# Strassen's scheme on two pairs of token blocks instead of one, with weights in stages of two chunks, in a kernel of attention and two expert layers

## The chip, the cores and the metric

The kernel runs on one core of a Trainium2 chip. The metric is the device time of the whole program in microseconds (us); lower is better. Times of several executions of the kernel before are given below, and one of its executions was profiled.

## The reference

Attention with a window of 32 over 512 local positions and 32 global ones (4 batches, 8 heads, head size 64), then two layers without gates, each a product, a squared ReLU and a product:

```python
def _moe_ref(x, w_in, w_out):          # x: 2176 tokens x 512 here, d_ff = 2048
    h = x @ w_in
    r = np.maximum(h, 0.0)
    return ((r * r) @ w_out).astype(np.float32)

attn_out = _attn_ref(...)              # softmax over window and global keys
x = attn_out.transpose(0, 2, 1, 3).reshape(B * S, H * D)     # 2176 x 512
x = _moe_ref(x, moe_w_in, moe_w_out)
return _moe_ref(x, moe2_w_in, moe2_w_out)
```

The weights arrive as 64-bit floats and are narrowed on the chip.

## The kernel before

**Precision.** Each product of the layers is made of three matmuls of a rounded part and a remainder: `three()` issues hi x hi, hi x lo and lo x hi (lines L575, L576, L577), and every operand that is used is first split in a high part (`xh`, `gh`, `whi`, `th`) by ScalarE and a low part (`xl`, `gl`, `wlo`, `tl`) by a subtraction. "A three" below is one such group.

**Tiling.** Tokens lie in five blocks of 256, 512, 512, 512 and 384 columns (blocks 0 to 4). The hidden size of 2048 is cut in 16 chunks of 128 per layer; the model size of 512 is four pieces `k` (into `w_in`) or `d` (out of `w_out`). A wave is four chunks of both weights, so there are 8 waves, wave 0 beside the attention. For one chunk, a block that goes the plain way needs 4 threes into `h` and 4 threes out of `w_out`.

**Strassen's scheme.** Blocks 1 and 2 are a pair from wave 1 on. For two chunks, `products` makes the same four results from 7 products of two threes, 14 threes instead of 16. For it `sums` combines two weight chunks into two more operands (slots `sa`, `sb`), and `tsums` combines the pair's inputs into three more (`t`, at the start of each layer). One running sum is kept in PSUM, copied out three times by ScalarE (`keep`) and added to by VectorE (`plus`, L707).

**Activation.** A plain result takes ScalarE's ReLU and square (L596, L597), VectorE's exact square (L599) and VectorE's remainder (L233). A staged result of the pair takes VectorE's square (L589), ScalarE's copy to `gh` (L591) and the remainder. Results of `w_out` are added into `y` by VectorE (L626): a plain block once in a wave, the pair's blocks twice.

**Weights.** `weight` loads a chunk (512 KB), and VectorE and ScalarE rebuild 32-bit floats from the halves of the 64-bit ones (L488 to L500); `split` writes `whi` and `wlo` of a slot. There are 12 slots.

**Order.** All instructions are given to a planner (`Plan`) with costs, a priority and what they read and write; it simulates the engines and always takes the ready instruction of the lowest priority number. The order that it prints is fixed when the program is built, and each engine then runs its own list in order. `CFG` holds the priorities, the order of the blocks in each wave, and a string per kind of step that deals its instances to engines in turn (A ScalarE, D VectorE, P GpSimd). In the attention part TensorE fills its pauses with wave 0.

Of the kernel before, what the change touches and what calls it, by code (L numbers as in the profile page):

```python
# [10 lines left out]
F32 = mybir.dt.float32  # L11
# [15 lines left out]
BLOCKS = [[0], [1, 2], [3, 4], [5, 6], [7]]  # L27
NB = [256, 512, 512, 512, 384]
OFF = [0, 256, 768, 1280, 1792]
UNIT_POS = {u: (b, 256 * j) for b, us in enumerate(BLOCKS) for j, u in enumerate(us)}  # L30
WAVES = 4
NSLOT = 12
PB = (1, 2)
CFG = {'sg': 'AAA',
 'tl': 'D',
 'tp': [495.69, 306.05],
 'order': ['340W', '3W04', 'W403', '4W30', 'W043', '0W43', '3W40'],
 'EARLY': 8,
 'ck': 'PPPP',
 'cq': 'P',  # L40
 'lo': 'DDD',
 'nm': 'APA',
 'ev': 'A',
 'yc': 'A',
 'wl': 'DDDD',
 'gl': 'D',
 'xh': 'AAA',
 'glob': [6, 7, 13, 15, 19, 26, 27, 29],
 'w0': -7.103,
 'w1': 56229.445,  # L50
 'moe': [850.402, 480.622, -326.592, -124.726, -387.48],
 'step': [0.1043, 0.0123, 0.0591, 0.0383, 0.0372],
 'NK': 3,
 'NQ': 2,
 'wa': 'ADDA',
 'lid': -6.29,
 'lmk': -11.49,
 'gbuf': '01',
 'lead': 14112208.283,
 'NM': 2,  # L60
 'NS': 3,
 'NPT': 2,
 'NV': 2,
 'lag': 6,
 'NR': 3,
 'NWR': 1,
 'NWT': 3,
# [4 lines left out]
 'O': ['O0']}  # L72
# [129 lines left out]
def kernel(ctx: ExitStack, tc: tile.TileContext, kl, ql, vl, gk, gv, win, wout, msk, idn, out):  # L202
# [47 lines left out]
    gh = tiles(big, "gh", 4, [128, 512], F32R)  # L250
    gl = tiles(big, "gl", 4, [128, 512], F32R)
# [24 lines left out]
    late_opened, tt_ = [], []  # L276
# [24 lines left out]
    def pair(j, prio):  # L301
# [31 lines left out]
        visit(P, scores, (M, ML, HQ, LQ), tuple(sk), 0.767)  # L333
# [48 lines left out]
        b, c0 = UNIT_POS[u]  # L382

        def after(P):
            split_out(b, [h2], xh[b][:, h2, c0:c0 + 256], xl[b][:, h2, c0:c0 + 256], ok, bank[ok][:, 0:256], 256, P)

        add("PE", 0.924, P(), pv, A + (("pt", pbs[0]), ("pt", pbs[1]), ("v", vb)), (ok,), mode="V")
        after(P)

    waiting = []  # L390

    def visit(P, scores, reads, writes, cost):

        if scores:
            add("PE", cost, P(), scores, ("arena",) + reads, writes, mode="S")
# [8 lines left out]
    def glob(n, prio):  # L404
# [3 lines left out]
        k, v = (yflat[3], yflat[4]) if gb == 0 else (yflat[2], yflat[1])  # L408
# [62 lines left out]
        c0 = 256 + 32 * bb  # L471
# [60 lines left out]
    def weights(w, prio, prio_step, step=1e-3):  # L532
# [16 lines left out]

        def chunk(kind, i):  # L550
            s, a = slot()
            res[kind].append(s)
            if prio_step:
                q[0] = prio + prio_step * (len(res["in"]) + len(res["out"]) - 1)
            return weight((win if kind == "in" else wout)[4 * w + i], s, P, a)

        if w == 0:
            for kind in ("in", "out"):
                for i in range(4):
                    chunk(kind, i)  # L560
            return res
        for p in range(2):
            t = [chunk("in", 2 * p + i) for i in range(2)]
            ss = [slot() for _ in range(2)]
            sums(t[0], t[1], [s for s, _ in ss], P, dict(ss))
            res["sum"].append([s for s, _ in ss])
            for i in range(2):
                chunk("out", 2 * p + i)
# [15 lines left out]
    def activate(P, f, nb, src, S, staged):  # L584

        a, l = gh[f][:, 0:nb], gl[f][:, 0:nb]
        if staged:
            r, R = src, S
# [4 lines left out]
        else:  # L593
            r, R = staging()
            r = r[:, 0:nb]
# [3 lines left out]
            add("DVE", dve(nb), P(), lambda: nc.vector.scalar_tensor_tensor(  # L599
                out=r, in0=src, scalar=0.0, in1=r, op0=ALU.max, op1=ALU.mult), (S,), (R,))  # L600
# [5 lines left out]
    def second(P, b, fs, slots, late, dfirst, stages):  # L606
# [11 lines left out]
        def finish(d):  # L618
# [3 lines left out]
            if begin:  # L622
                first = {1: (("gv", 1),), 2: (("gk", 1), ("gp", 1)), 3: (("gk", 0), ("gp", 0)), 4: (("gv", 0),)}.get(b, ())
# [3 lines left out]
            if end and layer == 0:  # L627
                if b == PB[1] and d < 2:
                    return
# [25 lines left out]
    def moe(W, layer, wave, b, prio, late, step=1e-3, free=False):  # L655
        nb = NB[b]
        c3 = 3 * pe_r(nb)
        q = [prio]

        def P():  # L660
            q[0] += step
            return q[0]

        for f in range(4):
            slot = W["in"][f]
            hk = take("h", CFG["h"] + CFG["S"] if late else CFG["h"])
            hp = bank[hk][:, 0:nb]
            for k in range(KD):
                add("PE", c3, P(), lambda k=k, slot=slot, hp=hp: three(
                    hp, wv(whi, slot)[:, k, :], wv(wlo, slot)[:, k, :], xh[b][:, k, :], xl[b][:, k, :], k == 0, k == KD - 1),  # L670
                    (("w", slot), ("x", b, k)), (hk,))
            activate(P, f, nb, hp, hk, False)
        second(P, b, range(4), W["out"], late, not late, (layer, wave == 0, wave == WAVES - 1))
        if free:
            release(*W["in"], *W["out"])
# [3 lines left out]
    tkey = lambda n, i: ("x", PB[1], i) if n == 1 else ("T", n, i)  # L679
# [238 lines left out]
```

## Time and profile before

| | |
|---|---|
| median of 3 runs | 892.65 us (891.47 to 893.81) |
| the profiled execution | 893.89 us |
| its span, from first to last instruction | 892.0 us |
| TensorE busy | 871.2 us |
| VectorE busy | 685.5 us |
| ScalarE busy | 428.9 us |
| GpSimd busy | 64.6 us |
| mean granted TensorE clock | 0.998 of full speed |

The busy time of an engine counts the time in which at least one of its instructions is under way; instructions of one engine overlap a little, so it is less than the sum of their durations. The profiled execution lies 1.24 us above the median of the runs.

### The profile page before, as it was taken

Reading aid. Unit: us, or ns where it says so; the run is one execution under the profiler, and the core shown is the slowest. Engines: PE = TensorE matmul, PEld = TensorE weight load, DVE = VectorE, ACT = ScalarE, POOL = GpSimd, SP = SyncE. Lnnn points to the kernel's source line nnn. Section 1 sums busy time; section 2 is a strip of 40 time slices with the busy share of each in tenths; the row PEclk is TensorE's granted clock in tenths of the full one; section 3 lists DMA queues with packets and bytes.
Section 4 is the critical chain, followed back from the end, with each engine's and each line's share of the span. In section 5 each row is a group of like instructions: output and inputs, shape, how many; then the busy total and the mean of one; then the engine's idle time right before and its main releaser. Section 6 shows DMA issues by size and latency. Waiting matters only on the chain.

```text
span 892.0 us, 14332 instructions
## 1 busy us (share of the span) xinstructions
PE 871.2 (98%) x5332; PEld 752.9 (84%) x5332; DVE 685.5 (77%) x1584; ACT 428.9 (48%) x996; POOL 64.6 (7%) x119
## 2 busy tenths in 40 slices
PE   5989999999999999999999999999999999999998
PEld 4878887788789988889989998889899888988898
DVE  5878889653797788897999988847885988494653
ACT  5879899984552333333435544425323432232221
POOL 3323243310000000000000000000000000000000
PEclk9999999999999999999999999999999999999999
DMA  8568644410202102111210112201111211011021
GB/s 307 178 209 273 206 127 136 129 32 1 71 1 71 48 0 63 56 48 49 71 47 25 48 48 71 71 25 32 64 48 48 58 61 48 25 47 48 1 96 60
DMA packets 28071, 67.93 MB, mean 76 GB/s; under 512 B 3168, under 2 KB 12512, under 8 KB 28000
## 3 DMA queue, kind: packets, MB, share of 16 engines
q1 hardware_dynamic: 28000, 67.01, 23.8%
q8 instruction: 42, 0.69, 0.3%
q14 instruction: 29, 0.24, 0.1%
HBM read 62.54 MB, written 4.46 MB: 75 GB/s over the span
## 4 chain that ended last, share of the span: by engine, by line
PE 92%; DVE 3%; DMA 2%; ACT 2%; issue 1%; SPq 0%; POOL 0%; POOLq 0%; DVEq 0%; ACTq 0%
PE h L575 7%; PE h L576 7%; PE h L577 7%; PE PT L575 6%; PE PT L577 6%; PE PT L576 6%; PE S L575 6%; PE S L577 6%; PE S L576 6%; PE Y L575 5%; PE Y L577 4%; PE Y L576 4%; PE O L378 4%; PE O L575 3%; PE O L577 3%; PE O L576 3%
## 5 line engine op out<-in xcount | busy, mean ns | idle before, releaser
L575 PE MATMUL h<-xh,whi 128*128 128x512 f32 (+2 forms) x298 | 108.2, 363 | 0.0
L576 PE MATMUL h<-xl,whi 128*128 128x512 f32 (+2 forms) x298 | 105.3, 353 | 0.0
L577 PE MATMUL h<-xh,wlo 128*128 128x512 f32 (+2 forms) x298 | 105.2, 353 | 0.0
L233 DVE TENSOR_TENSOR gl<-r,gh 128x512 fp32r<-128x512 f32 (+2 forms) x160 | 96.8, 608 | 9.9 <-ACT gh L591 7.9
L577 PE MATMUL PT<-gh,wlo 128*128 128x512 f32 (+2 forms) x288 | 102.6, 356 | 0.0
L575 PE MATMUL PT<-gh,whi 128*128 128x512 f32 (+2 forms) x288 | 102.6, 356 | 0.0
L576 PE MATMUL PT<-gl,whi 128*128 128x512 f32 (+2 forms) x288 | 102.6, 356 | 0.0
L524 ACT ACTIVATE whi<-wt 128x512 fp32r<-128x512 f32 x92 | 57.3, 627 | 60.9 <-DVE wt L500 38.9
L233 DVE TENSOR_TENSOR wlo<-wt,whi 128x512 fp32r<-128x512 f32 x92 | 62.8, 686 | 26.1 <-ACT whi L524 25.9
L575 PE MATMUL S<-xh,whi 128*128 128x512 f32 (+2 forms) x230 | 80.2, 349 | 1.0 <-DVE r L599 1.0
L577 PE MATMUL S<-xh,wlo 128*128 128x512 f32 (+2 forms) x230 | 80.1, 348 | 0.0
L576 PE MATMUL S<-xl,whi 128*128 128x512 f32 (+2 forms) x230 | 80.1, 348 | 0.0
L575 PE MATMUL Y<-gh,whi 128*128 128x512 f32 (+2 forms) x208 | 76.8, 369 | 2.5 <-ACT y L218 2.5
L577 PE MATMUL Y<-gh,wlo 128*128 128x512 f32 (+2 forms) x208 | 74.7, 359 | 0.0
L576 PE MATMUL Y<-gl,whi 128*128 128x512 f32 (+2 forms) x208 | 74.7, 359 | 0.0
L596 ACT ACTIVATE r<-h 128x512 f32<-128x512 f32 (+2 forms) x67 | 34.3, 512 | 73.4 <-PE h L577 73.0
L597 ACT ACTIVATE gh<-r 128x512 fp32r<-128x512 f32 (+2 forms) x118 | 63.9, 542 | 10.4 <-PE O L577 6.6
L347 ACT ACTIVATE s<-s,mn 128x224 f32<-128x224 f32 x128 | 60.3, 474 | 17.0 <-DVE mn L342 16.1
L575 PEld LDWEIGHTS h<-xh,whi 128*128 128x128 f32 x298 | 56.4, 189 | 8.3 <-issue 0.3
L576 PEld LDWEIGHTS h<-xl,whi 128*128 128x128 f32 x298 | 56.5, 190 | 6.4 <-DVE xl L400 0.2
L577 PEld LDWEIGHTS h<-xh,wlo 128*128 128x128 f32 x298 | 56.4, 189 | 6.4
L596 ACT ACTIVATE r<-S 128x512 f32<-128x512 f32 (+2 forms) x51 | 25.7, 504 | 73.8 <-PE S L577 65.7
(109 smaller groups left out, 2011.5 us busy)
## 6 DMA issues: line engine op xcount, KB each, us to landing
wraw<-win SPq DMA_DIRECT2D x32, 512.0 KB, 3.6
wraw<-wout SPq DMA_DIRECT2D x32, 512.0 KB, 3.6
v<-vl SPq DMA_DIRECT2D x32, 224.0 KB, 2.8
rk<-kl SPq DMA_DIRECT2D x32, 192.0 KB, 3.5
y<-gk SPq DMA_DIRECT2D x8, 672.0 KB, 5.4
y<-gv SPq DMA_DIRECT2D x8, 640.0 KB, 6.7
rq<-ql SPq DMA_DIRECT2D x32, 128.0 KB, 3.0
out<-y SPq DMA_DIRECT2D x12, 256.0 KB, 2.0
```

What stands on the lines that cost most here:

```text
L233: add("DVE", dve(n), prio, lambda: nc.vector.tensor_tensor(out=get(out_), in0=get(a), in1=get(b), op=ALU.subtract), reads, writes, lock=True)
L347: add("Activation", 0.48, P(), lambda t=t, sb=sb: nc.scalar.activation(out=st[sb][:, t, :], in_=st[sb][:, t, :], func=AF.Exp, bias=mn[sb][ ...
L378: nc.tensor.matmul(out=bank[ok][64 * e:64 * e + 64, 128 * t:128 * t + 128], lhsT=vt[vb][:, 128 * k + 64 * e:128 * k + 64 * e + 64], rhs=pt ...
L524: nc.scalar.activation(out=whi[slot], in_=tf, func=AF.Copy)
L575: nc.tensor.matmul(out=out_, lhsT=hi, rhs=xhi, start=start, stop=False, skip_group_check=again)
L576: nc.tensor.matmul(out=out_, lhsT=hi, rhs=xlo, start=False, stop=False, skip_group_check=again)
L577: nc.tensor.matmul(out=out_, lhsT=lo, rhs=xhi, start=False, stop=stop, skip_group_check=again)
L596: add("Activation", act(nb), P(), lambda: nc.scalar.activation(out=r, in_=src, func=AF.Relu), (S,), (R,))
L597: add("Activation", act(nb) + 0.04, P(), lambda: nc.scalar.activation(out=a, in_=r, func=AF.Square), (R,), (("gh", f),))
```

## The change

Blocks become 256, 512, 512, 448 and 448 columns. Blocks 1 and 2 are pair A, blocks 3 and 4 pair B, and both go through `w_in` by `products`; block 0 alone goes the plain way. After wave 0, which keeps its four plain chunks, there are 14 stages of two chunks (6 in the first layer, 8 in the second) instead of 7 waves of four. A stage has the three parts 0, A and B in an order of its own, and the `w_out` part of a pair's second block is issued after the next part's products (`pending`). Every block's `w_out` results are now added to `y` once in a stage. Weight slots are 8 instead of 12, staging tiles (`r`) 8 instead of 3, temporary weight tiles 4 instead of 3, tiles of transposed probabilities (`pt`) 6 instead of 2, and tiles for `k` 2 instead of 3. The ring of GpSimd's own DMAs, which the kernel does not use, shrinks to 256 bytes. `CFG` deals steps anew: 8 of the 32 roundings of `k` (`ck`) go to ScalarE and 16 to VectorE, 21 of the 32 remainders of `k` (`lo`) go to GpSimd, 27 of the evictions of attention results (`xh`) go to VectorE, and the exact square goes to ScalarE for all staged results and for four plain ones out of five.

```diff
-BLOCKS = [[0], [1, 2], [3, 4], [5, 6], [7]]
-NB = [256, 512, 512, 512, 384]
-OFF = [0, 256, 768, 1280, 1792]
+NB = [256, 512, 512, 448, 448]
+OFF = [0, 256, 768, 1280, 1728]
-WAVES = 4
-NSLOT = 12
-PB = (1, 2)
+PAIRS = {"A": (1, 2), "B": (3, 4)}
+STAGES = KF // 2
-CFG = {'sg': 'AAA',
- 'order': ['340W', '3W04', 'W403', '4W30', 'W043', '0W43', '3W40'],
+CFG = {'sg': 'A',
- 'ck': 'PPPP',
+ 'ck': 'APDD',
- 'lo': 'DDD',
+ 'lo': 'PDP',
- 'xh': 'AAA',
- 'glob': [6, 7, 13, 15, 19, 26, 27, 29],
- 'w0': -7.103,
+ 'xh': 'DADDA',
+ 'glob': [0, 2, 5, 8, 16, 17, 23, 27],
+ 'w0': 5694.227,
- 'NK': 3,
+ 'NK': 2,
- 'NPT': 2,
+ 'NPT': 6,
- 'NR': 3,
+ 'NR': 8,
- 'NWT': 3,
+ 'NWT': 4,
+ 'order': ['0AB', 'A0B', 'AB0', '0BA', 'A0B', '0BA', 'B0A', 'B0A', 'B0A', 'A0B', '0AB', 'A0B', '0AB', 'BA0'],
+ 'NSLOT': 8,
+ 'gf': 'AAAAD',
+ 'gs': 'A'}
...
-            for j in range(3):
-                tt_.append([lp.tile([128, 2, 512], F32R, name=f"t{k}{j}") for k in "hl"])
+            for g, (b, _) in PAIRS.items():
+                for n in (2, 3, 4):
+                    tt_[g, n] = [lp.tile([128, 2, NB[b]], F32R, name=f"t{g}{k}{n}") for k in "hl"]
...
-        if staged:
-            r, R = src, S
+        r, R = (src, S) if staged else staging()
+        r = r[:, 0:nb]
+        if staged and pick("gs") == "D":
...
-            add("DVE", dve(nb), P(), lambda: nc.vector.scalar_tensor_tensor(
-                out=r, in0=src, scalar=0.0, in1=r, op0=ALU.max, op1=ALU.mult), (S,), (R,))
+            if staged or pick("gf") == "A":
+                add("Activation", act(nb) + 0.04, P(), lambda: nc.scalar.activation(out=r, in_=r, func=AF.Square), (), (R,))
+            else:
+                add("DVE", dve(nb), P(), lambda: nc.vector.scalar_tensor_tensor(
+                    out=r, in0=src, scalar=0.0, in1=r, op0=ALU.max, op1=ALU.mult), (S,), (R,))
...
-    for lw in range(1, 2 * WAVES):
-        layer, wave = divmod(lw, WAVES)
-        order = CFG["order"][lw - 1]
-        for n, j in enumerate(order):
-            prio, last = 100 * lw + 10 * n, n == len(order) - 1
-            if j == "W":
-                wino(W, layer, wave, prio, free=last)
-            else:
-                moe(W, layer, wave, int(j), prio, True, free=last)
-        if lw == WAVES - 1:
-            tsums(100 * lw + CFG["tp"][1], True)
-        if lw + 1 < 2 * WAVES:
-            W = weights(lw + 1, 1000, 0)
+            W = weights((KF * layer + 2 * p, KF * layer + 2 * p + 1), 1000, 0, True)
+            if stage == 0:
+                for i, g in enumerate(PAIRS):
+                    tsums(g, CFG["tp"][i], False)
...
+                if j == "0":
+                    for i in range(2):
+                        first(P, W, 0, i, mine[i], True)
+                    rest, blocks = None, (0,)
+                else:
+                    rest, blocks = products(W, j, P, mine), PAIRS[j]
+                    if j == pairs[-1]:
+                        release(*W["sum"])
+                if n == len(order) - 1:
+                    release(*W["in"])
+                if pending:
+                    pending()
+                if rest:
...
+                    rest(P, theirs)
+                    second(P, blocks[0], mine, W["out"], True, True, stages)
...
-    nc = _bacc.Bacc("TRN2", target_bir_lowering=False, num_devices=1)
+    nc = _bacc.Bacc("TRN2", target_bir_lowering=False, num_devices=1, dynamic_dma_scratch_size=256)
```

Three places in the order of instructions show what moves. The first is TensorE's list in the middle of the layers, where block 3 meets `w_in`. `h0`, `h1`, `S0` and `S1` are PSUM banks; the number behind the underscore tells tiles of one program apart. Before, a chunk (`whi4`, then `whi5`) meets the block's own parts `xh3` and `xl3`, 512 columns wide:

```order
L575 MATMUL S0_143<-xh3_67,whi4_98 128x512
L576 MATMUL S0_143<-xl3_72,whi4_98 128x512
L577 MATMUL S0_143<-xh3_67,wlo4_106 128x512
L575 MATMUL S1_144<-xh3_67,whi5_99 128x512
L576 MATMUL S1_144<-xl3_72,whi5_99 128x512
L577 MATMUL S1_144<-xh3_67,wlo5_107 128x512
```

In the changed kernel, in the middle of a part B, a combined weight (slot 2) meets the pair's combined input `tB2` and then block 4's own:

```order
L565 MATMUL S1_153<-tBh2_2837,whi2_102 128x448
L566 MATMUL S1_153<-tBl2_2838,whi2_102 128x448
L567 MATMUL S1_153<-tBh2_2837,wlo2_110 128x448
L565 MATMUL h1_150<-xh4_68,whi2_102 128x448
L566 MATMUL h1_150<-xl4_73,whi2_102 128x448
L567 MATMUL h1_150<-xh4_68,wlo2_110 128x448
```

For two chunks the blocks 3 and 4 had 16 threes each here; they now have 14 together with the same columns as one block of 448, and all their matmuls are 448 wide.

The second place is the start of TensorE's list, behind the scores of the first pair of heads (L330, L334 scores; L365, L369 transposes; L382 product with `v`; L422 scores of the global queries). Before, the scores of the second pair follow at once, then the transposes of the first, then the third pair's scores:

```order
L330 MATMUL S0_143<-hk1_116,lq1_122 128x224
L330 MATMUL S1_144<-hk1_116,lq1_122 128x224
L330 MATMUL S0_143<-lk1_118,hq1_120 128x224
L330 MATMUL S1_144<-lk1_118,hq1_120 128x224
L365 MATMUL PT0_145<-ident_139,s0_123 112x128 x4
L365 MATMUL PT1_146<-ident_139,s1_124 112x128 x4
L330 MATMUL S0_143<-hk0_115,hq0_119 128x224
L330 MATMUL S1_144<-hk0_115,hq0_119 128x224
```

In the changed kernel the first pair's last scores are followed by scores of a global step and by the first pair's own transposes and product:

```order
L334 MATMUL S0_152<-lk0_122,hq0_124 128x224
L334 MATMUL S1_153<-lk0_122,hq0_124 128x224
L422 MATMUL S0_152<-y1_75 128x272 x2
L369 MATMUL PT0_154<-ident_148,s0_128 112x128 x4
L369 MATMUL PT1_155<-ident_148,s1_129 112x128 x4
L422 MATMUL S1_153<-y1_75 128x272 x2
L382 MATMUL O0_156<-pt0_131,v0_137 64x128
L382 MATMUL O0_156<-pt1_132,v0_137 64x128
```

The global steps have moved ahead, and the second pair's scores stand behind the first pair's product. On the DMA queue the first weight chunk, which was the 9th load, is now the 17th, behind four loads of the global steps.

The third place is VectorE's list where the first layer ends and the inputs of the second are combined (`y` are the layer's results, `tl` and `xl` remainders, L759 and L725 the sums of `tsums`, L599 the exact square). Before, the one pair's sums stand between the work of a plain block of 384 columns:

```order
L759 TENSOR_TENSOR y2_76<-y2_76,y1_75 128x512
L633 TENSOR_TENSOR xl2_71<-y2_76,xh2_66 128x512
L233 TENSOR_TENSOR tl1_2735<-y2_76,th1_2734 128x512
L599 SCALAR_TENSOR_TENSOR r2_89<-S0_143,r2_89 128x384
L233 TENSOR_TENSOR xl2_71<-y2_76,xh2_66 128x512
L233 TENSOR_TENSOR gl0_83<-r2_89,gh0_79 128x384
```

In the changed kernel pair B's sums stand between the work of pair A's last part of the first layer, and pair A's sums follow some 40 instructions later:

```order
L725 TENSOR_TENSOR y4_78<-y4_78 128x448
L625 TENSOR_TENSOR xl4_73<-y4_78,xh4_68 128x448
L695 TENSOR_TENSOR r0_87<-r0_87,S0_152 128x512
L235 TENSOR_TENSOR tBl3_2840<-y4_78,tBh3_2839 128x448
L725 TENSOR_TENSOR y4_78<-y4_78,y3_77 128x448
L725 TENSOR_TENSOR y3_77<-y3_77,y4_78 128x448
L725 TENSOR_TENSOR y4_78<-y4_78 128x448
L725 TENSOR_TENSOR y3_77<-y3_77 128x448
L235 TENSOR_TENSOR gl0_83<-r0_87,gh0_79 128x512
```

There are two sets of such sums instead of one, and of the exact squares one is left in VectorE's list around them.

## Rows read from the trace of the kernel before

**Rows 1.** The page: span, and each engine's busy time, share and instructions.

```profile
span 892.0 us, 14332 instructions
PE 871.2 (98%) x5332; PEld 752.9 (84%) x5332; DVE 685.5 (77%) x1584; ACT 428.9 (48%) x996; POOL 64.6 (7%) x119
```

**Rows 2.** Busy time by stretch: length, engines' busy us (instructions), TensorE clock, DMA share, GB/s.

```profile
0.00:20.00 20.00, 9.59 (x57) 7.14 (x59) 11.19 (x40) 9.43 (x28) 6.85 (x16) 1.00 0.90 313
0.00:215.50 215.50, 201.29 (x1895) 163.82 (x1895) 155.84 (x633) 173.44 (x527) 64.60 (x119) 0.99 0.52 165
260.00:888.00 628.00, 626.98 (x3237) 552.36 (x3236) 491.15 (x883) 232.89 (x427) 0.00 (x0) 1.00 0.15 48
450.00:500.00 50.00, 50.00 (x277) 45.67 (x276) 48.77 (x92) 24.77 (x47) 0.00 (x0) 1.00 0.10 32
```

**Rows 3.** TensorE's waits over the whole span: us in total, times, longest.

```profile
PE S L330 <- DVE mn L342: 6.3, 3, 5.3
...
PE O L378 <- DMA v<-vl: 2.7, 1, 2.7
PE Y L575 <- ACT y L218: 2.5, 4, 0.7
PE S L575 <- DVE r L599: 1.0, 1, 1.0
```

**Rows 4.** Timeline of TensorE at three widths: start us, duration, line, tiles.

```profile
319.73 0.39 PE L575 MATMUL h<-xh,whi 128*128 128x512 f32 x1
319.96 0.39 PE L576 MATMUL h<-xl,whi 128*128 128x512 f32 x1
...
432.17 0.33 PE L575 MATMUL Y<-gh,whi 128*128 128x384 f32 x1
432.35 0.33 PE L576 MATMUL Y<-gl,whi 128*128 128x384 f32 x1
...
406.09 0.28 PE L575 MATMUL h<-xh,whi 128*128 128x256 f32 x1
406.21 0.28 PE L576 MATMUL h<-xl,whi 128*128 128x256 f32 x1
```

**Rows 5.** Groups by line, one shape apart: the pair's combined inputs on TensorE.

```profile
L575 PE MATMUL S<-th,whi 128*128 128x512 f32 x42 | 16.3, 389 | 0.0
L575 PE MATMUL h<-th,whi 128*128 128x512 f32 x42 | 16.3, 389 | 0.0
```

**Rows 6.** Groups by line, one shape apart, and timeline: prices off TensorE.

```profile
L626 DVE TENSOR_TENSOR y<-y,PT 128x256 f32<-128x256 f32 x12 | 4.6, 418 | 0.0
L589 DVE SCALAR_TENSOR_TENSOR r<-r 128x512 f32<-128x512 f32 x42 | 28.8, 686 | 0.4
L488 DVE TENSOR_SCALAR wt<-wraw 128x512 uint32<-128x512 uint32 x64 | 27.2, 426 | 21.7 <-DMA wraw<-win 13.7 <-DMA wraw<-wout 7.7
L597 ACT ACTIVATE gh<-r 128x512 fp32r<-128x512 f32 x54 | 34.0, 630 | 1.4 <-PE Y L577 0.5
L226 POOL TENSOR_SCALAR hk<-rk 128x384 fp32r<-128x384 f32 x32 | 18.4, 574 | 56.6 <-PE S L330 28.5 <-issue 13.1 <-DMA rk<-kl 7.6
...
472.56 0.68 DVE L626 TENSOR_TENSOR y<-y,Y 128x512 f32<-128x512 f32 x1
473.16 0.68 DVE L626 TENSOR_TENSOR y<-y,PT 128x512 f32<-128x512 f32 x1
```

**Rows 7.** Timeline of the start: first steps of GpSimd, VectorE and TensorE.

```profile
6.76 0.40 POOL L226 TENSOR_SCALAR hq<-rq 128x256 fp32r<-128x256 f32 x1
6.77 0.80 DVE L233 TENSOR_TENSOR lk<-rk,hk 128x384 fp32r<-128x384 f32 x1 [1.91 <-POOL hk L226]
10.75 0.39 DVE L342 CUSTOM_DVE_ANT_0 s<-S,masks 128x224 f32<-128x224 f32 x1 [2.84 <-DMA masks<-msk]
12.00 0.55 DVE L233 TENSOR_TENSOR lk<-rk,hk 128x384 fp32r<-128x384 f32 x1
22.18 0.56 PE L575 MATMUL h<-xh,whi 128*128 128x256 f32 x1
```

More of the change, by code (lines that the diff above doesn't have):

```diff
@@ L380, in pv @@
                                          rhs=pt[pbs[e]][0:112, 128 * k:128 * k + 128], start=c == 0, stop=c == 1)
-        b, c0 = UNIT_POS[u]
-        def after(P):
-            split_out(b, [h2], xh[b][:, h2, c0:c0 + 256], xl[b][:, h2, c0:c0 + 256], ok, bank[ok][:, 0:256], 256, P)
         add("PE", 0.924, P(), pv, A + (("pt", pbs[0]), ("pt", pbs[1]), ("v", vb)), (ok,), mode="V")
[L388 to L395, printed above, removed]
+        for b in range(5):
+            lo, up = max(256 * u, OFF[b]), min(256 * u + 256, OFF[b] + NB[b])
+            if lo < up:
+                c, o = slice(lo - OFF[b], up - OFF[b]), bank[ok][:, lo - 256 * u:up - 256 * u]
+                split_out(b, [h2], xh[b][:, h2, c], xl[b][:, h2, c], ok, o, up - lo, P)
     def split_out(b, ks, hi, lo, ok, o, n, P):
@@ L548, in weights @@
         res = {"in": [], "out": [], "sum": []}
[L550 to L568, printed above, removed]
+        n = 0
+        for kind, src in (("in", win), ("out", wout)):
+            done = []
+            for c in chunks:
+                if prio_step:
+                    q[0] = prio + prio_step * n
+                n += 1
+                s, a = slot()
+                res[kind].append(s)
+                done.append(weight(src[c], s, P, a))
+            if with_sums and kind == "in":
+                ss = [slot() for _ in range(2)]
+                res["sum"] = [s for s, _ in ss]
+                sums(done[0], done[1], res["sum"], P, dict(ss))
         return res
@@ L653, in second, with first, tkey, th @@
                         finish(d)
-    def moe(W, layer, wave, b, prio, late, step=1e-3, free=False):
-        nb = NB[b]
+    def first(P, W, b, n, f, late):
+        nb, slot = NB[b], W["in"][n]
         c3 = 3 * pe_r(nb)
[L658 to L679, printed above, removed]
-    th = lambda n, i: xh[PB[1]][:, i, :] if n == 1 else tt_[n - 2][0][:, i, :]
-    tl = lambda n, i: xl[PB[1]][:, i, :] if n == 1 else tt_[n - 2][1][:, i, :]
-    def products(W, p, P):
-        b0, b1 = PB
+        hk = take("h", CFG["h"] + CFG["S"] if late else CFG["h"])
+        hp = bank[hk][:, 0:nb]
+        for k in range(KD):
+            add("PE", c3, P(), lambda k=k: three(
+                hp, wv(whi, slot)[:, k, :], wv(wlo, slot)[:, k, :], xh[b][:, k, :], xl[b][:, k, :], k == 0, k == KD - 1),
+                (("w", slot), ("x", b, k)), (hk,))
+        activate(P, f, nb, hp, hk, False)
+    def tkey(g, n, i):
+        return ("x", PAIRS[g][1], i) if n == 1 else ("T", g, n, i)
+    def th(g, n, i):
+        return xh[PAIRS[g][1]][:, i, :] if n == 1 else tt_[g, n][0][:, i, :]
+    def tl(g, n, i):
+        return xl[PAIRS[g][1]][:, i, :] if n == 1 else tt_[g, n][1][:, i, :]
+    def products(W, g, P, f):
+        b0, b1 = PAIRS[g]
         nb = NB[b0]
         c3 = 3 * pe_r(nb)
-        f0, f1 = W["in"][2 * p:2 * p + 2]
-        sa, sb = W["sum"][p]
+        f0, f1 = W["in"]
+        sa, sb = W["sum"]
         kb, ka, kc = (take("h", CFG["h"] + CFG["S"]) for _ in range(3))
@@ L804 @@
     GPOS = CFG["glob"]
-    W = weights(0, CFG["w0"], CFG["w1"])
+    W = weights(range(4), CFG["w0"], CFG["w1"], False)
     for j in range(NI // 2):
@@ L831 @@
+    pending()
     with tc.manual_schedule():
```

134 lines of the change are left out of this document (73 added, 61 removed).

## The prediction, made before the changed kernel ran

> **What bounds the kernel now.** I began with the engines' shares on the page [rows 1]. TensorE is busy for 871.2 of 892.0 us; the reader is to see that the next engine, VectorE, has 77%, so work taken from VectorE, ScalarE or GpSimd is worth nothing by itself. A share hides where the pauses lie, so the table by stretch came next [rows 2]. Up to 215.5 us, where the last attention product runs, TensorE is busy for 201.3 us and pauses for 14.2. From 260 to 888 us it is busy for 626.98 of 628 us: in the layers nothing makes it wait. Its list of waits says the same [rows 3]: 6.3 us at the start for VectorE's `mn`, 2.7 for a load of `v`, 2.5 for ScalarE's copies out of the one bank `Y0` in wave 0, 1.0 for `r`. So the kernel is as long as TensorE's list, plus some 21 us of pauses: 14.2 of them before 215.5 us and 4 after the last matmul. The change is worth what it takes off the list, less any new pause.
>
> **The pace of TensorE.** Busy matmuls overlap, so their durations (0.39 us) are no price; I took the distance from start to start [rows 4]. It is 0.227 us at 512 columns, 0.173 at 384 and 0.120 at 256. The three lie on one line: 0.053 us for 128 columns. No row shows 448 columns; the neighbours bound it by 0.173 and 0.227, and the line gives 0.200, which I take because the width lies midway between two points of a line that a third confirms. A three thus costs 0.68, 0.60, 0.52 and 0.36 us at 512, 448, 384 and 256 columns.
>
> The Trainium skill, "TensorE: Matmul & The Clock Gate", section "Back-to-back issue gap", gives N/2.4 + 2.5 ns for an isolated matmul, which is 215.8 ns at 512 columns; the trace does not agree, with 227 ns. By that formula the saving worked out next would be 15.8 instead of 16.8 us.
>
> **The change, part by part.**
>
> *TensorE in the layers.* Before, a wave of four chunks has, at 512 columns, 16 threes of block 3 and 28 of the pair into `w_in` and 48 of three blocks out of `w_out`; that is 92 x 0.68 = 62.6 us. That one pair takes the scheme for seven waves is in the counts [rows 5]: 84 hi x hi matmuls on `th`, 12 in a wave. Block 4 has 32 x 0.52 = 16.6 and block 0 has 32 x 0.36 = 11.5, in all 90.7 us. After, two stages have 28 + 32 threes of pair A at 0.68 (40.8), 28 + 32 of pair B at 0.60 (36.0) and block 0 with 11.5, in all 88.3. The difference is 2.4 us, and seven times that **16.8 us**. TensorE's list has 84 matmuls fewer, as 7 x 12 asks. With the bounds of the 448-wide price it would be 16.8 + 7 x 180 x 0.0267 = 50 us gained, or 17 lost; three points on a line leave both little chance. Wave 0 costs the same in both cuts (32 threes of each block; 0.68 + 0.52 = 0.60 + 0.60).
>
> *VectorE in a stage.* At 512 columns two starts lie 0.60 us apart and an instruction lasts 0.68 [rows 6]; I take 0.08 off each duration for one behind the other: 0.60, 0.53 (between 0.60 and 0.34), 0.34 for 512, 448, 256 columns and 0.34 for the narrow form L488. A stage asks for four chunks at 2.85 (11.4), the weight sums and their remainders (2.5), ten `gl` (5.2), six `plus` (3.4), twenty additions to `y` (10.4) and some 0.5 of exact squares: 33.4 of 44.2 us. The twenty additions are the new part: plain blocks pay twice as often. It is paid with the exact squares that leave (28.8 us for the 42 staged ones alone, [rows 6]). VectorE stays at three quarters. It ran at 48.77 of 50 us around the turn of the layers and TensorE did not wait at all [rows 2], so this load is no bound. ScalarE gets 229 more squares at 0.63 us or less, some 125 us on top of 429; at 555 of 875 it stays below two thirds. Both are priced at nothing, covered by TensorE's list; without the cover the squares would cost their 125 us.
>
> *Eight slots.* I followed each slot in the changed order and summed TensorE's pace between the last use of its content and the first use of the next: 13 us or more everywhere but at two places, 3.0 us (first chunk after wave 0) and 8.4. What must fit in is one ScalarE rounding (0.63) and one VectorE remainder (0.68), if the rebuilding is done ahead in the `wt` tiles. Nothing.
>
> *The start.* The first matmul of wave 0 came at 22.18 us [rows 7]. Its chunk was the 9th load, behind 1.6 MB; now it is the 17th, behind 4.8 MB. At the 313 GB/s of the first 20 us [rows 2] that is 10 us later. In that time TensorE has more of its own: an estimate by the matmuls that stand ahead of the first three, at 0.1 us for one of scores or values and 0.23 for one of global scores, is 14.7 us now against 6.2. I take the difference, **+2 us** of pause; the bounds are -4 (the early pause for the masks till 10.75 us gets filled by global scores) and +8 (all of the delay but that pause).
>
> *The turn of the layers.* Between the first addition to block 0's `y` and the last `tA` remainder VectorE has 125 instructions, 77 us by durations and 67 back to back; TensorE's list between the same two points is 73 us. It fits with 6 us to spare, which VectorE's own waits may eat. I take **+1.5 us**, between 0 and 8.
>
> *The rest.* In wave 0 other matmuls stand between the groups that wait for `Y0`: **-1 us** of the 3.5, between 0 and -3. GpSimd's empty ring moves nothing: all loads are SyncE's.
>
> Sum against the profiled execution's 893.89: 893.89 - 16.8 + 2 + 1.5 - 1 = 879.6. That execution lay 1.24 us above the median of the runs, so I forecast **878 us** for the median.
>
> **The rivals.**
>
> *The attention part gets longer.* GpSimd now makes 21 remainders of `k`. The trace shows that it and VectorE hinder each other: VectorE's `lk` took 0.80 us with a GpSimd instruction beside it and 0.55 without [rows 7]. GpSimd's price for it is unknown: 0.57 us (its mean for `hk`, as wide and with one input, [rows 6]) to twice that. If each one stops VectorE for 1.1 us that is 23 us, against 13 that VectorE no longer spends on them. The roundings and evictions dealt to VectorE use those 13 up, so it would have about 180 of 217 us instead of 156 of 215.5 [rows 2], still below TensorE. But the order is fixed, and TensorE waits at each score that comes late. I price it at half of the 23 us: 890. Chance 0.12.
>
> The Trainium skill, "SBUF — State Buffer", section "Who interferes with whom", says that a VectorE instruction with two SBUF inputs and a GpSimd instruction that reads SBUF lock each other out entirely. The 0.80 against 0.55 us agree with a lock of 0.25 us.
>
> *The attention part gets shorter.* Six `pt` tiles, eight `r` tiles and the new dealing may close half of the 14.2 us of pauses: 893.89 - 16.8 - 7 - 1.24 = 869. Against it: the pauses lie where first data are missing, not where steps queue. Chance 0.12.
>
> *The turn of the layers stalls.* If VectorE's waits there reach 15% of 67 us, TensorE stands for some 4 to 10 us: 882 to 887. Chance 0.1.
>
> *Slower: weights late at every stage.* With 8 slots the two sums can only be written once the last pair has finished with the old ones, and weight work has the lowest priority (1000). If TensorE waited 2 us for them at each of 14 stages, that is +28: 905. From 1.1 us a stage on the gain is gone. Against it stand the 13 us windows. Chance 0.06.
>
> **How the numbers follow.** The forecast has a chance of 0.6, with its own range of 872 to 884 from the bounds of the start and of the turn. The range of 8 in 10 takes in the stalled turn and most of the longer attention: 869 to 887. A change of 0.3% (2.7 us) is about what a measurement of this kernel can tell from none. Faster than 890 are the forecast, the shorter attention, the stalled turn and a half of the longer attention: 0.88. Within 0.3% is most of the rest of that case, 0.05; slower are its tail and the late weights, 0.07.
>
> **What would show it.** TensorE's matmuls at 448 columns start 0.200 us apart; its busy time is 854 us; from some 260 us to the end it is never idle but at the turn of the layers (about 450 us), where a wait for `tA` or `tB` of a few us may stand. The first three of wave 0 comes near 27 us. VectorE is busy for about 690 us, ScalarE for about 555. Wrong would be: waits on `wlo` at stage starts (slots), TensorE's pauses before 215 us well over 16 us (attention), or VectorE at full load through the layers.

## The result and the profile after

The changed kernel took 885.19 us (median of 4 runs, 884.31 to 888.09) against 893.23 us for the kernel before (median of 4, 891.47 to 893.85). The ratio is 0.9919, with a 95% interval of 0.989 to 0.9947: 8.0 us faster, where the forecast was 878 us, some 15 us faster. A second measurement, further down, gave 885.32 us and 0.9916 (0.9886 to 0.9946). The profiled execution took 884.31 us.

The page of the changed kernel, span and engines, to be read beside [rows 1]:

```profile
span 882.5 us, 14400 instructions
PE 860.1 (97%) x5248; PEld 743.1 (84%) x5248; DVE 697.0 (79%) x1619; ACT 551.3 (62%) x1234; POOL 70.8 (8%) x116
```

TensorE has the 84 matmuls fewer that the forecast counted, and VectorE (690 forecast, 697 measured) and ScalarE (555 and 551) came out about as said. But TensorE's busy time fell by 11.1 us, to 860.1, and not by 16.8 to 854. That is the main miss; the pauses, span less busy time, went from 20.8 to 22.4 us, +1.6 where the sum had +2.5. Even the 11.1 us are not all the change's: TensorE ran at half clock for a while in the kernel before, which the first of these two rows shows; the second is the same stretch in the changed kernel:

```profile
54.00:57.40 3.40, 3.29 (x21) 2.88 (x22) 2.85 (x14) 2.16 (x9) 0.72 (x1) 0.50 0.16 33
54.00:57.40 3.40, 3.40 (x38) 2.77 (x36) 2.93 (x8) 3.12 (x10) 1.23 (x3) 1.00 0.95 333
```

The granted clock of 0.50 (1.2 instead of 2.4 GHz) begins as a wait of 2.7 us for `v` ends, one of those in [rows 3]. An estimate from that row: at the full clock the 3.29 us of work would have taken about half, so 1.6 of the 11.1 us are the clock's, and at one clock TensorE's list became some 9.5 us shorter.

Busy time by stretch of the changed kernel, beside [rows 2]:

```profile
0.00:20.00 20.00, 10.01 (x60) 7.87 (x61) 8.84 (x37) 8.25 (x22) 5.49 (x13) 1.00 0.86 297
0.00:218.70 218.70, 201.85 (x1907) 162.73 (x1907) 163.30 (x650) 178.71 (x527) 70.82 (x116) 1.00 0.52 165
260.00:878.00 618.00, 616.82 (x3138) 544.11 (x3137) 496.23 (x903) 345.30 (x654) 0.00 (x0) 1.00 0.17 50
500.00:550.00 50.00, 50.00 (x254) 44.10 (x253) 49.85 (x89) 40.52 (x81) 0.00 (x0) 1.00 0.11 32
```

The second row ends with the last attention product: 218.7 us instead of 215.5, with 16.9 us of pauses instead of 14.2. The third says that in the layers nothing makes TensorE wait (1.2 us in 618). The fourth is the turn of the layers, where VectorE writes the `tB` and `tA` remainders of the second layer from 504 to 549 us: TensorE is never idle, though VectorE has 49.85 of 50 us. So VectorE is full there, with nothing to spare, and still on time.

TensorE's waits in the changed kernel (us in total, times, longest), beside [rows 3]:

```profile
PE S L422 <- DVE sm L356: 4.7, 2, 4.3
PE S L334 <- POOL hq L228: 4.0, 1, 4.0
PE h L566 <- DVE xl L396: 2.3, 1, 2.3
PE PT L369 <- ACT s L220: 1.4, 2, 0.9
PE S L565 <- ACT r L220: 1.4, 2, 0.7
```

There is no wait for `wlo` (the eight slots) and none for `tA` or `tB` (the turn). The waits for the copies out of `Y0`, 2.5 us before, have shrunk to 0.2. New is one wait of 2.3 us for `xl`, which an experiment takes up. The pace is next: the timeline of TensorE at 448 and at 512 columns, beside [rows 4]:

```profile
404.62 0.36 PE L565 MATMUL Y<-gh,whi 128*128 128x448 f32 x1
404.81 0.36 PE L566 MATMUL Y<-gl,whi 128*128 128x448 f32 x1
405.01 0.37 PE L567 MATMUL Y<-gh,wlo 128*128 128x448 f32 x1
405.22 0.36 PE L565 MATMUL PT<-gh,whi 128*128 128x448 f32 x1
...
411.70 0.36 PE L567 MATMUL O<-gh,wlo 128*128 128x448 f32 x1
411.91 0.39 PE L565 MATMUL S<-xh,whi 128*128 128x512 f32 x1
412.13 0.39 PE L566 MATMUL S<-xl,whi 128*128 128x512 f32 x1
```

From 404.62 to 411.70 us stand 35 steps of 448 columns: 7.08 / 35 = 0.202 us each. From 300 to 870 us their mean is 0.2037, without seven steps that took over 30 ns more. The forecast had taken 0.200. There are 1452 such matmuls in the kernel.

### The profile page after: what moved, and what is told of

It reads as the page before. It is cut to its first block, busy times and chain, and to the rows that moved or that the text cites. A ratio compares the mean times of both kernels' runs of the same rounds, so it can differ in the third digit from the quotient of the medians.

```text
span 882.5 us, 14400 instructions
## 1 busy us (share of the span) xinstructions
PE 860.1 (97%) x5248; PEld 743.1 (84%) x5248; DVE 697.0 (79%) x1619; ACT 551.3 (62%) x1234; POOL 70.8 (8%) x116
## 4 chain that ended last, share of the span: by engine, by line
PE 84%; ACT 6%; DVE 5%; DMA 3%; issue 1%; SPq 0%; POOL 0%; ACTq 0%; DVEq 0%
PE h L565 7%; PE h L566 7%; PE h L567 7%; PE PT L566 6%; PE PT L565 6%; PE PT L567 6%; PE S L565 5%; PE S L566 5%; PE S L567 5%; PE Y L565 4%; PE Y L566 4%; PE Y L567 4%; PE O L566 3%; PE O L567 3%; PE O L565 3%; PE O L382 2%
## 5 line engine op out<-in xcount | busy, mean ns | idle before, releaser
L235 DVE TENSOR_TENSOR gl<-r,gh 128x448 fp32r<-128x448 f32 (+2 forms) x160 | 96.6, 610 | 59.2 <-ACT r L589 57.9
L566 PE MATMUL PT<-gl,whi 128*128 128x448 f32 (+2 forms) x288 | 103.5, 359 | 0.0
L565 PE MATMUL PT<-gh,whi 128*128 128x448 f32 (+2 forms) x288 | 103.4, 359 | 0.0
L567 PE MATMUL PT<-gh,wlo 128*128 128x448 f32 (+2 forms) x288 | 103.3, 359 | 0.0
L586 ACT ACTIVATE gh<-r 128x448 fp32r<-128x448 f32 (+2 forms) x160 | 89.1, 562 | 2.4 <-PE Y L567 0.2
L589 ACT ACTIVATE r<-r 128x448 f32<-128x448 f32 (+2 forms) x145 | 82.2, 568 | 3.8
L618 DVE TENSOR_TENSOR y<-y,PT 128x448 f32<-128x448 f32 (+2 forms) x130 | 75.5, 600 | 9.2 <-PE PT L567 8.9
L565 PE MATMUL S<-xh,whi 128*128 128x448 f32 (+2 forms) x184 | 65.5, 356 | 0.0
L566 PE MATMUL S<-xl,whi 128*128 128x448 f32 (+2 forms) x184 | 65.3, 355 | 0.0
L567 PE MATMUL S<-xh,wlo 128*128 128x448 f32 (+2 forms) x184 | 65.1, 354 | 0.0
```

Source lines behind the costliest of these rows:

```text
L235: add("DVE", dve(n), prio, lambda: nc.vector.tensor_tensor(out=get(out_), in0=get(a), in1=get(b), op=ALU.subtract), reads, writes, lock=True)
L565: nc.tensor.matmul(out=out_, lhsT=hi, rhs=xhi, start=start, stop=False, skip_group_check=again)
L566: nc.tensor.matmul(out=out_, lhsT=hi, rhs=xlo, start=False, stop=False, skip_group_check=again)
L567: nc.tensor.matmul(out=out_, lhsT=lo, rhs=xhi, start=False, stop=stop, skip_group_check=again)
L586: add("Activation", act(nb) + 0.04, P(), lambda: nc.scalar.activation(out=a, in_=r, func=AF.Square), (R,), (("gh", f),))
L589: add("Activation", act(nb) + 0.04, P(), lambda: nc.scalar.activation(out=r, in_=r, func=AF.Square), (), (R,))
```

## The experiments

My theory after the result: the 448-column price was wrong, because it does not lie on the line through 512, 384 and 256 columns. The rivals: the steps are slowed by what runs beside them; the order was made for the wrong price; and, for the rest, the deals between the engines hold the gain back.

**Widths alone.** A kernel of matmuls only, 60 in a row at each width, with all of the reference's work left out.

```diff
+    for n in (512, 480, 448, 432, 416, 400, 384, 352, 320, 288, 256, 192):
+        for i in range(60):
+            nc.tensor.matmul(out=b[:, 0:n], lhsT=w[:, 128 * (i % 4):128 * (i % 4) + 128], rhs=x[:, n * (i % 4):n * (i % 4) + n], ...)
```

> The kernel leaves out all of the reference's work: it is 60 matmuls at each of twelve widths between 512 and 192 columns, each with a weight load of its own, first with TensorE alone and then, at 512, 448, 384 and 256, while VectorE and ScalarE work without pause in SBUF. Width theory (a 448-wide matmul costs more than the line through 512, 384 and 256 columns, which gives 0.200 us): in the lone part 448 columns start about 0.203 us apart, 512 0.227, 384 0.173, 256 0.120. Company theory (448-wide ones lose time to the other engines or to waits of the new stages): alone they start 0.200 us apart, and 0.203 or more only in the second part.

Groups of TensorE by width in this kernel (count, busy us, mean ns of one); a stretch is some 0.17 us longer than its starts, since the last matmul has nothing behind it:

```profile
L43 PE MATMUL b<-x,w 128*128 128x448 f32 x180 | 37.0, 365 | 0.0
L43 PE MATMUL b<-x,w 128*128 128x384 f32 x180 | 31.7, 334 | 0.0
L43 PE MATMUL b<-x,w 128*128 128x480 f32 x60 | 13.2, 379 | 0.0
L43 PE MATMUL b<-x,w 128*128 128x416 f32 x60 | 11.4, 350 | 0.0
```

The 448 columns stood in three stretches: (37.0 - 0.5) / 180 = 0.2028 us; 384 the same way 0.1733. From start to start, mean of the last 40 of a stretch, and the line's value behind it: 512 0.2267; 480 0.2167 (0.2133); 448 0.2026 (0.2000); 432 0.1967 (0.1933); 416 0.1880 (0.1867); 400 0.1833 (0.1800); 384 0.1733; 352 0.1617 (0.1600); 320 0.1467; 288 0.1300 (0.1333); 256 0.1200; 192 0.1117 (0.0933). So 448 costs 2.7 ns more than the line, with TensorE alone. With VectorE and ScalarE at work beside it, it was 0.2027, and with the inputs 512 columns apart in SBUF 0.2027 too: the company theory falls, and so does the place of the inputs in SBUF.

**The cut alone.** The kernel before with the changed kernel's block widths. Of the rest it takes only what the widths ask for: attention results that cross a block's edge are copied out in two parts, and the buffers of the global steps lie in other blocks.

```diff
-NB = [256, 512, 512, 512, 384]
+NB = [256, 512, 512, 448, 448]
```

> The kernel before with one part of the change alone: blocks of 256, 512, 512, 448 and 448 columns, one pair by Strassen's scheme, waves of four chunks, 12 slots, nothing else. On the line of widths TensorE's list stays as long as before, so the company theory expects 893 us, within 3 us. Width theory: 1536 matmuls of 448 columns at 0.0039 us more each, 6.0 us more TensorE time (877 us busy), about 899 us.

900.69 us, ratio 1.008 (1.0062 to 1.0099): 7.1 us slower, near the 6 of the width theory. The lone prices give 768 x (2 x 0.2027 - 0.2267 - 0.1733) = 4.1 us; on the line it would be nothing. The rest is not the width's: the planner made a new order here too. TensorE is busy for 875.4 us, 4.2 more than before, but that agrees with 4.1 by luck: without the half clock of the kernel before it would be some 5.8, of which the attention has about 1. What settles the price is the pace inside this kernel, which keeps the old scheme. A stretch in the layers with 192 steps of 448 columns:

```profile
671.87 0.37 PE L574 MATMUL S<-xh,whi 128*128 128x448 f32 x1
672.08 0.36 PE L575 MATMUL S<-xl,whi 128*128 128x448 f32 x1
...
710.58 0.36 PE L576 MATMUL O<-gh,wlo 128*128 128x448 f32 x1
710.79 0.28 PE L574 MATMUL S<-xh,whi 128*128 128x256 f32 x1
```

(710.79 - 671.87) / 192 = 0.2027 us, the lone price.

**Other widths in the pairs.**

```diff
-NB = [256, 512, 512, 448, 448]
+NB = [384, 512, 512, 384, 384]
```

> The changed kernel with pair B cut to 384 and 384 columns and block 0 grown to 384. By the line of widths its list costs 88.64 us for two stages against 88.32, so the company theory expects TensorE's list 2.2 us longer than in the changed kernel: 887 us. Width theory: 448 columns cost 0.204, so the changed kernel's two stages cost 89.0 and the cut at 384 saves 0.4 in each of seven and 0.75 in wave 0: 3.4 us less TensorE time (857 us busy), about 882 us. The planner's order changes everywhere, which may move the pauses by some 3 us either way; TensorE's busy time tells the theories apart better than the whole.

902.23 us, ratio 1.0104 (1.0081 to 1.0128): both theories missed by 15 to 20 us, and no price of a width explains it. By the lone prices its list is some 1.7 us shorter than the changed kernel's. But the planner had made a new order: the attention's own steps (all matmuls that are not of the layers, from start to start, with their waits) took 149.9 us in sum instead of 138.7, and a halt of 3.4 us at 267 us went with a granted clock of 0.83 from 260 to 280 us, part of that stretch at 1.2 instead of 2.4 GHz. So I first had to know what a new order costs by itself.

**The order by itself.** Two kernels that change one price in the planner and no work: one is told the true 448-column price (its order differs in a few places after 260 us), one has 5 ns more for each ScalarE instruction (its order differs from about 25 us on).

```diff
-    return max(n + 32, 2 * m + 6) / 2400
+    return max(n + (38.4 if n == 448 else 32), 2 * m + 6) / 2400
```

> The changed kernel, and only the planner's table of costs is told that a 448-wide step takes 0.203 us instead of 0.200; the work is the same, the order differs in a few places after 260 us. Width theory (the missing gain is the chip's own price of 448 columns, not an order made for a wrong price): 885 us within 2, TensorE busy 860. Rival (the order made with the wrong price is what loses the gain): 881 us or less, and fewer waits after 260 us. It also measures what a small change of order alone does to the time.

```diff
 def act(n):
-    return 0.055 + 0.835 * n / 1000
+    return 0.060 + 0.835 * n / 1000
```

> The changed kernel, and only the planner's price of a ScalarE instruction is 5 ns higher: no work changes, the order changes from about 25 us on. Theory 'tuned order' (the attention's order is good only for the numbers it was made with; four edits that made it anew all had their attention steps at 150 to 153 us instead of 139): 893 to 899 us, attention steps near 150 us. Rival 'edits' (what those edits cost is their own): 885 to 888 us, attention steps 139.

The first took 886.38 us, ratio 0.9922 (0.9899 to 0.9945), TensorE busy 860.9: the wrong price in the planner lost nothing. The second took 898.09 us, ratio 1.0049 (1.0027 to 1.0072): 13 us lost with the same work, attention steps 148.5 us. A nudge of 5 ns in one price is enough to lose the attention's good order. That may be most of the 17 us of the 384-column kernel, and it means that a whole time of a kernel whose attention was ordered anew says little about its edit. In the nudged kernel the clock's rows show part of the loss:

```profile
40.00:60.00 20.00, 18.15 (x179) 14.68 (x176) 16.87 (x72) 17.38 (x53) 7.60 (x11) 0.85 0.80 255
54.00:64.00 10.00, 9.44 (x64) 7.39 (x65) 6.39 (x25) 7.25 (x25) 3.85 (x7) 0.50 0.62 204
```

The granted clock is 0.50 from 54 to 64 us, in a stretch with pauses of 1.1 and 0.6 us; in the changed kernel it is 1.00 in every 20 us. The mean granted clock of the profiled execution was 0.992 of full speed here and in the 384-column kernel, and 1.000 in the changed kernel: 0.008 x 898 us, an estimate of 7 us of either loss. What the rest is was not tested.

**The squares.** The changed kernel moved exact squares from VectorE to ScalarE, which I had priced at nothing. Back on VectorE, all of them:

```diff
- 'gf': 'AAAAD',
- 'gs': 'A'}
+ 'gf': 'D',
+ 'gs': 'D'}
```

> The changed kernel with all exact squares back on VectorE. The prediction's sum gives VectorE 33.4 of 44.2 us in a stage, with the squares back some 38.4. If that is right VectorE still has room and the time stays at 885 us within 3 us, VectorE busy for some 740 us and ScalarE for some 440. Rival: VectorE was near its limit and the move of the squares carried the change; then TensorE waits for gl or r in the stages and the time rises by 8 us or more.

912.98 us, ratio 1.0217 (1.019 to 1.0243), VectorE at 84%. The head of its list of TensorE's waits:

```profile
PE Y L567 <- DVE wlo L235: 9.3, 2, 8.9
```

Two kernels split it in time, with the squares back from the second layer stage on (about 300 us), or only up to there:

```diff
-        if staged and pick("gs") == "D":
+        if staged and now[0] >= 1:        # the other: now[0] < 1
```

> The changed kernel with the second squares (r<-r of ScalarE) back on VectorE from the second stage of the layers on (about 300 us); the attention part and the first layer stage keep their order. Theory 'early': what the full move back cost (28 us) lies before 300 us, in the attention products and in the 9-us halt near 270 us, and VectorE has room in the layers: 885 to 890 us, no new TensorE wait above 1 us after 300 us, 512-wide steps 0.228 apart. Rival 'spread': in the layers too VectorE's row is late with gl and the adds: 897 us or more, with waits of TensorE for VectorE or ScalarE after 300 us of 9 us in sum, as near 547 to 567 us of the kernel with all squares on VectorE, and the granted clock below 1 there.

> The changed kernel with the second squares back on VectorE only in wave 0 and in the first layer stage (up to about 300 us). Theory 'early': nearly the whole 28 us return, 905 to 912 us, with the steps of attention (those that are no layer matmuls) at 150 us instead of 139 and a halt near 270 us behind VectorE. Rival 'spread': half of it or less, 890 to 898 us.

Late: 893.49 us, ratio 0.9994 (0.9978 to 1.001), 8 us over the changed kernel, between the two theories. The profiled execution fell behind the changed kernel's by 3.6 us up to 99 us, where nothing was changed, which is chance, and by most of the rest at the turn of the layers:

```profile
500.00:550.00 50.00, 44.91 (x205) 37.64 (x203) 49.33 (x88) 26.89 (x50) 0.00 (x0) 0.96 0.05 14
```

VectorE is as full as in the changed kernel, but now it is late: TensorE waits 2.7 us for `wlo` and 1.1 for `whi`, and the granted clock of the stretch is 0.96. Early: 907.16 us, ratio 1.0147 (1.0119 to 1.0174), 22 us over, as the theory 'early' said. But its attention had been ordered anew (its steps took 150.2 us), and the nudged kernel lost 13 us by that without any square moved. The rest is the halt of 8.9 us for `wlo`, which also stands in the run with all squares moved:

```profile
260.00:280.00 20.00, 11.14 (x60) 10.25 (x59) 19.83 (x39) 10.82 (x22) 0.00 (x0) 0.74 0.00 0
```

VectorE has 19.83 of 20 us and TensorE 11.14, and the clock of the stretch fell to 0.74. In VectorE's list `wlo` stands behind the last of the first layer's `tB` remainders; it writes that one at 275.0 us here and at 264.3 in the changed kernel. So I put the squares on VectorE with TensorE's list kept word for word. For a staged result VectorE's square takes the place of ScalarE's ReLU, and ScalarE then only copies; for a plain one it stands where ScalarE's square had stood:

```diff
-            add("Activation", act(nb), P(), lambda: nc.scalar.activation(out=r, in_=src, func=AF.Relu), (S,), (R,))
+            D = lambda: nc.vector.scalar_tensor_tensor(out=r, in0=r, scalar=0.0, in1=r, op0=ALU.max, op1=ALU.mult)
+            add("Activation", act(nb), P(), D if staged else lambda: ...Relu..., (S,), (R,))
```

> The changed kernel with all second squares on VectorE, as in the run that was 28 us slower, but each at the place in the program that ScalarE's had, so that TensorE's list stays word for word. Theory 'order' (most of the 28 us was the attention's order made anew): attention steps 139 us, 893 us with the 8 us that the late squares cost. Rival 'load' (VectorE at 84% is late whatever the order): 905 us or more, TensorE waiting for VectorE or for gl and xl before 300 us.

920.31 us, ratio 1.031 (1.027 to 1.0349): my theory 'order' falls for the squares. The attention steps stay near their old sum (141.6 us), as it said, but VectorE's load shows all along the layers:

```profile
PE Y L566 <- DVE gl L235: 9.9, 14, 1.7
...
270.00:878.00 608.00, 592.01 (x2964) 512.57 (x2964) 539.69 (x993) 230.76 (x428) 0.00 (x0) 1.00 0.15 45
```

From 270 to 878 us VectorE has 540 of 608 us (89%; the changed kernel, from 260 us, 80%) and TensorE pauses for 16 us, for `gl` above all. The execution is 5.9 us behind the changed kernel's at the last attention product and 34.1 at the end; part of the first is a clock of 0.83 from 80 to 100 us. An order made for that load lost less than the old one with the load put in: 912.98 with a new attention, and only 893.49 in the late kernel, which keeps the attention's order and moves 119 of the same 145 squares. So the 35 us are the price in an order that does not know of the load.

**GpSimd's remainders.** The rival on record was that its 21 `lk` hold VectorE back. First the deal of before:

```diff
- 'ck': 'APDD',   'lo': 'PDP',
+ 'ck': 'PPPP',   'lo': 'DDD',
```

> The changed kernel with GpSimd's share of the attention's splits dealt as before (all of the first copies on GpSimd, all of the remainders lk on VectorE). Rival on record (GpSimd's 21 remainders hold VectorE back): attention shorter by 3 to 4 us, 881 us. Theory of the prediction (they take work off VectorE and hold nothing): no shorter, 885 us or more; VectorE busy 21 x 0.4 = 8 us more in the first 219 us, and whatever it is late with then shows as TensorE's waits there.

898.93 us, ratio 1.0054 (1.0033 to 1.0075), attention steps 153.2 us: the attention was ordered anew, and by the nudged kernel nearly all of the 13.7 us can be order, so this run decides nothing. Then the 21 on VectorE with every other list the same:

```diff
-            add("Pool", 0.25 + 0.0021 * n, prio, lambda: nc.gpsimd.tensor_tensor(
+            add("Pool", 0.25 + 0.0021 * n, prio, lambda: nc.vector.tensor_tensor(
```

> The changed kernel with GpSimd's 21 remainders lk (1.11 us each there) on VectorE (0.59 us each), at the same places of the program, all other lists word for word the same. Rival on record (GpSimd's remainders hold VectorE back): 881 us or less, attention over by 215 us. Theory of the prediction (they take work off VectorE, 12 us of its first 219): 885 to 890 us, attention not over before 219 us.

886.76 us, ratio 0.9933 (0.9906 to 0.9959): not faster, 1.6 us over the changed kernel, so the rival (881 us or less) falls.

**The wait for `xl`.** In the changed kernel VectorE's list waits at 86.7 us for a weight's DMA, and `xl`, ready at 87.4 us, stands behind it; the timeline there, with the idle time before a row and what ended it:

```profile
86.55 0.17 DVE L357 RECIPROCAL sm<-sm 128x2 f32<-128x2 f32 x1
90.58 0.43 DVE L484 TENSOR_SCALAR wt<-wraw 128x512 uint32<-128x512 uint32 x1 [3.87 <-DMA wraw<-wout]
90.93 0.42 DVE L396 TENSOR_TENSOR xl<-O,xh 128x256 fp32r<-128x256 f32 x1
...
91.40 0.50 PE L566 MATMUL h<-xl,whi 128*128 128x512 f32 x1 [2.26 <-DVE xl L396]
```

Two kernels move that conversion back in VectorE's list: its first step by two rows, then all four steps behind the five rows that were ready. The last run is the changed kernel again, on the chip of the second.

```diff
-        for op in plan.order():
+        seq = plan.order()
+        seq.insert(558, seq.pop(553))          # the second: also 561, 565, 568, to behind 571
+        for op in seq:
```

> The changed kernel with one instruction of VectorE's list moved back by two: the first step of the weight conversion (wt<-wraw, L484) that waits 3.87 us for its DMA at 86.7 to 90.6 us now stands behind xl<-O and y<-S,masks, which were ready at 87.4 and 88.1 us. Theory (a halt at the head of VectorE's list holds TensorE's h<-xl by 2.26 us, and TensorE is the bound): 882.9 us, 2.3 below the changed kernel; no h L566 <- xl wait left. Rival (the time comes back behind it, since the conversion or the next weight load is then late): 885 us, and a new wait of 2 us within the next 20 us. Either way faster than before.

> The changed kernel with all four steps of that weight conversion (L484, L486, L488, L491) behind the five rows of VectorE that were ready before its DMA landed (xl, y<-S,masks, gmx, one mn, gsm); every other list is word for word the same. Theory 'head of the list' (the 1.8 us that came back at 93 us was gmx behind L486): no wait of TensorE above 0.5 us between 88 and 97 us, 882.7 us, 2 to 2.5 below the changed kernel run beside it. Rival (something else is late next in each case, so the time comes back again): within 1 us of the changed kernel.

> The changed kernel itself once more, to stand beside the run with the four moves on the same chip: 885.2 us within 1 by both theories, a wait of 2.3 us for xl at 91 us.

One row moved: 884.47 us, ratio 0.9913 (0.988 to 0.9946). The wait for `xl` is gone, and within 4 us another stands in its place, since `gmx`, on which this `y` depends, was still behind the conversion:

```profile
95.09 0.66 PE L448 MATMUL PT<-ident,y 128*128 128x128 f32 x4 [1.75 <-POOL y L443]
```

Four rows moved: 883.84 us, ratio 0.9891 (0.9867 to 0.9914), the lowest median of all, beside 885.32 us for the changed kernel, whose wait for `xl` was 1.6 us this time. The wait for `y` is gone too, and 1.3 us came back for an `xh` at 95.6 us. The medians lie 1.5 us apart, but the intervals overlap, and the two profiled executions do not show a gain: their spans are 883.4 and 882.3 us. Against the first profile of the changed kernel, the four moves are 1.0 us late at the first matmul of wave 0 (34.2 against 33.2 us) and still 0.8 late at the last attention product. So the runs show that the wait moves, and not that taking it away saves time; neither theory is decided.

## Why the prediction was wrong, point by point

- **The step that failed: "the line gives 0.200, which I take because the width lies midway between two points of a line that a third confirms".** The step costs 0.2027 us, alone, beside busy engines and in the old scheme. 1452 x 2.7 ns = 3.9 us of the term of -16.8 are lost by that. The prediction had seen that no row shows 448 columns, and gave bounds, but then said that three points left them little chance. It did not ask whether the line holds between its points.
- **The rest of that term.** It measured -11.1, so 5.7 us are missing, or some 7.3 at one clock, since the half clock of the kernel before flatters the change by 1.6. Behind the 3.9 stand two small things. From 300 to 870 us both widths take about 1 ns more in the changed kernel than elsewhere (448: 203.7 against 202.7 ns alone; 512: 227.9 against 226.9 ns before), some 2300 steps: 2.3 us. And twelve steps there took 37 to 360 ns more each, 1.6 us in sum, where the kernel before has none. In the kernel with late squares on VectorE 448 stayed at 202.7. What causes either stays open. So the wrong price is shown, and it is about half of what the term lacks.
- The count was right: 84 matmuls fewer, two threes in each of 14 stages. (The section on the change gives blocks 3 and 4 "16 threes each" into `w_in` for two chunks; it is 8 each, 16 together, against 14.)
- **Start: +2 forecast, nothing measured.** In the first 40 us TensorE is busy for 29.59 us before and 29.61 after. The first three of wave 0 came at 33.2 us, not near 27; TensorE had other work meanwhile. The pauses up to the last attention product did grow by 2.7 us, but that this is near +2 is luck: 2.3 of it is the wait for `xl`, which no step had priced, and other small waits came, while the waits for `v` (2.7 us) and `Y0` (2.5, priced at -1) all but went.
- **Turn of the layers: +1.5 forecast, nothing measured.** But the "6 us to spare" were not there: VectorE was full for 50 us, and the squares put back at this place made TensorE wait. It lies at 500 to 550 us, not "about 450".
- **Eight slots: nothing, as forecast.** Two kernels with a fuller VectorE halted for 9 us right after wave 0, near the place with a window of 3.0 us, but for a `wlo` that VectorE wrote late, not shown to be for a slot.
- **"VectorE stays at three quarters ... no bound": right for what was built**, with 79%, but the mean hid the turn. And the squares that leave are no side effect at a price of nothing: to put them back cost 8 us (119 of 145, in an order made for it) to 35 us (all, in place). The prediction counted VectorE's load after the move and gave the relief no price.
- **The two executions.** Spans differ by 9.5 us. The one profiled before lay 0.7 us above its median, the one after 0.9 below, so the medians differ by 8.0. The forecast of 878 was 7 us low: 4.7 by its terms (5.7 in TensorE's list, less 0.9 in the pauses), and 2.1 because it took the changed kernel's median to lie 1.24 us below the profiled execution, where it lay 0.9 above.
- **The range.** 885.19 us lies outside the forecast's own 872 to 884 and inside the wide 869 to 887. That the wide one holds it is luck: its upper end was set by the stalled turn and the longer attention, and neither is what happened.
- The rivals: GpSimd's remainders did not hold the attention up; the shorter attention, the stalled turn and late weights did not occur. The saving by the formula for an isolated matmul comes to 15.9 us, not 15.8.

## What to carry to other kernels

A price for a size that no row shows is an unknown until it is measured, even between points on a line: a kernel of 60 matmuls in a row would have told it. Compare the granted clocks of two executions before their busy times. Where an order is made by a planner with tuned numbers, compare whole times only of kernels that keep the order (put the changed instruction in the old place), or measure first what a nudge without any change of work costs; here it was 13 us, more than the gain under study. An engine's mean share does not say whether it is free: VectorE at 79% held nothing up, though it was full for 50 us at the turn, and three kernels at 84%, each with the load at other places of its list, lost 8, 28 and 35 us (the 28 with a new attention order in it). A row that waits for a DMA at the head of an engine's list holds what is ready behind it, but to take one such wait away need not save its time.

## What the runs showed of the hardware that was not expected

TensorE's step at these fp32r shapes is no straight line in the columns: 512, 384, 320 and 256 lie on 0.0533 us per 128 columns, while 480, 448, 432, 416, 400 and 352 cost 1.3 to 3.4 ns more, 288 costs 3.3 ns less, and 192 columns take 0.1117 us instead of 0.0933. At 448 the distances repeat in fives, from 0.199 to 0.207 us. Why these widths lie off the line is not shown.

The granted clock of the 20-us stretch was 0.91, 0.83 and 0.74 where TensorE halted for 2.7, 3.4 and 8.9 us. A halt can thus cost more than its length. But the length alone does not tell: in the changed kernel it was 1.00 around the 2.3 us for `xl`, while in the kernel with squares in place 0.83 stood around 2.6 us for the same `xl`, and in the nudged kernel the clock was 0.50 for 10 us around pauses of 1.1 and 0.6 us.
